# A range check on the row sums of a fused attention and FFN kernel, with a second path behind a branch

## The chip, the cores and the metric

The kernel runs on one core of one Trainium2 chip. The metric is device time in microseconds (us), the median of several runs. Beside it stands one execution taken by the hardware profiler; its span goes from the first to the last instruction of the program.

## What is computed

Eight sequences of 576 tokens with 8 heads of 64 are cut into chunks of 64 tokens. Each chunk attends to itself alone; the result goes through a multiplicative feed-forward network. Cut to what matters:

```python
scores = scale * np.matmul(q_c, k_c.transpose(0, 1, 2, 4, 3))
scores = scores - np.max(scores, axis=-1, keepdims=True)
attn = np.exp(scores)
attn = attn / (np.sum(attn, axis=-1, keepdims=True) + 1e-09)
out = np.matmul(attn, v_c)
# x: out as [4608 tokens, 512]; w1, w2: [512, 1024]; w3: [1024, 1024]; w_out: [1024, 512]
h = (x @ w1) * (x @ w2) @ w3
return h @ w_out
```

The inputs q, k and v are normal numbers times 0.1.

## The kernel before, in words

The 4608 tokens are worked in 18 parts p of 256 tokens (two units u of 128), and, from the products with w1 and w2 on, in 9 groups g = p // 2 of 512 tokens. The order of the work is written out by hand: the string ORDER names steps, each a letter with numbers, and the last lines of the kernel run them one after the other. Every instruction of a step is pinned in program order on its engine, so ORDER sets the queue of each engine. The steps that matter here:

- `q`, `k`, `v`, `i`, `o`, `h` load inputs and weights, issued by GpSimd (line 95). `T` (L197) transposes q and k on VectorE. `G` and `H` move tiles between partitions with DMAs that SP issues (line 189, `move`).
- `S`: scores on TensorE (all matmuls are recorded on line 92). `E` (L230): exp on ScalarE, straight from PSUM and without a maximum subtracted. `P`: products with v; a column of ones in v gives each row's sum beside them. `N` (L257, L260): VectorE takes the reciprocal of the sums (`rc`, 128x8) and multiplies. `X` (L272, L280): transposes for the network.
- `A`, `B`: products with w1 and w2 for eight slices j of the 1024 columns, `C` (L326): ScalarE copies the first out of PSUM into `a_sb`, `M` (L341): VectorE multiplies it with the second into `ab`. I write (12,5) for slice 5 of the group whose first part is 12.
- `V`, `W`, `Z` fold w3 and w_out into one matrix w3o, once. `O`: product of `ab` with it. `Y` (L371): ScalarE copies the result into `o_sb`; `Q`: SP stores it. The last part, O17, goes in three pieces (L364): two copies on ScalarE, and the last quarter on VectorE.

The sums, the scores, the pairs of products and the outputs share four PSUM tiles (`ps`, bufs=4) that rotate; `a_sb` has three buffers, `rc` two. The end of the kernel, in the order of ORDER, is the network of groups 12, 14 and 16 with the outputs between them: all attention is done before A12.1. After ORDER each engine branches to a closing block: SP waits on all semaphores, the engines meet, GpSimd clears the semaphores, and they meet again (recorded on line 449).

## Time and profile before

| what | value |
|---|---|
| median of 3 runs | 244.39 us (244.31 to 244.80) |
| span of the profiled execution | 243.1 us |
| granted TensorE clock | 1.000 |
| TensorE matmul busy | 225.9 us |
| VectorE busy | 153.7 us |
| ScalarE busy | 85.1 us |
| last matmul ends | 239.9 us |
| last copy (VectorE, L364) | 239.97, takes 0.42 us |

The runs are of the whole program; the profiled execution's time is known as its span, and what lies around it shows as the difference to the runs, 1.2 us. Engines are named PE (TensorE matmul), PEld (its weight load), DVE (VectorE), ACT (ScalarE), POOL (GpSimd) and SP (SyncE); a q behind a name is that engine's sequencer. In a timeline a row is start, duration, engine, line, operation and, in brackets, the idle time before it and what ended it. In a window table each pair is the busy time of an engine with its count, then the granted clock, the DMA engines' share and GB/s. In the list of a line, three numbers with slashes are the shortest, median and longest duration in ns, followed by the first and last start.

### The profile page before, as it was taken

The page shows a single profiled execution, that of the slowest core. Times are in us where ns is not written, and L with a number is a line of the kernel's source. Part 1 is how long each engine was busy: PE and PEld are TensorE (multiplying, and loading weights), DVE is VectorE, ACT ScalarE, POOL GpSimd, SP SyncE. Part 2 cuts the span into 40 slices and gives each one's busy share as a digit, 9 for nine tenths or more (in the row PEclk, how much of TensorE's full clock was granted, in tenths as well). Part 3 has the DMA queues.
Part 4 walks back from the last instruction along what each step waited for, and adds up shares of the span by engine and source line. Part 5 has one row for each costly group of instructions (what it writes and reads, how often), then busy time and mean ns, then how long its engine had stood idle before and what let it go on. Part 6 is the DMA issues. An engine that isn't in the chain of part 4 may idle for free.

```text
span 243.1 us, 6347 instructions
## 1 busy us (share of the span) xinstructions
PE 225.9 (93%) x2731; PEld 120.3 (49%) x2753; DVE 153.7 (63%) x232; ACT 85.1 (35%) x116; POOL 83.3 (34%) x112
## 2 busy tenths in 40 slices
PE   1299989999999979999999999999999999999994
PEld 1247868864545444444444444444444444444443
DVE  1856799689899578999998899918440332143000
ACT  2412323423333343534326335162332332332322
POOL 8847974665986444773260240000000000000000
PEclk9999999999999999999999999999999999999999
DMA  7999999999999999999999893735502200400244
GB/s 179 179 185 180 186 168 199 196 193 170 154 172 218 226 228 252 173 219 192 209 237 213 251 137 83 173 89 203 145 0 89 86 0 0 175 0 1 86 173 173
DMA packets 93595, 37.63 MB, mean 155 GB/s; under 512 B 75008, under 2 KB 86528, under 8 KB 93568
## 3 DMA queue, kind: packets, MB, share of 16 engines
q0 software_dynamic: 82592, 18.88, 83.9%
q1 hardware_dynamic: 9936, 17.83, 24.8%
q10 hardware_dynamic: 1040, 0.52, 0.8%
q8 instruction: 21, 0.34, 0.6%
q14 instruction: 6, 0.05, 0.1%
HBM read 38.80 MB, written 9.44 MB: 198 GB/s over the span
## 4 chain that ended last, share of the span: by engine, by line
PE 70%; DMA 16%; DVE 5%; SPq 3%; issue 2%; POOL 2%; ACT 0%; DVEq 0%; POOLq 0%
PE ab_ps L92 38%; PE o_ps L92 23%; PE w_ps L92 6%; DMA w<-in_moe_w_dram 4%; DMA qkm<-qkT 3%; DMA xt<-xm 3%; DMA qk<-in_k_dram 3%; DMA qk<-in_q_dram 3%; SPq L189 3%; PE s_ps L92 2%; PE pv L92 2%; DVE qkT L197 2%; DVE xn L260 1%; DVE ab L341 1%; POOL vbuf L95 1%
## 5 line engine op out<-in xcount | busy, mean ns | idle before, releaser
L92 PE MATMUL ab_ps<-xt,w 128*128 128x512 bf16 (+1 forms) x681 | 126.8, 342 | 1.4 <-DVE xt L272 0.9
L92 PEld LDWEIGHTS <-w 128*128 128x128 bf16 x704 | 67.3, 98 | 55.4 <-DVE xt L272 1.4
L341 DVE TENSOR_TENSOR ab<-a_sb,ab_ps 128x512 bf16<-128x512 f32 x71 | 47.8, 674 | 43.5 <-ACT a_sb L326 43.3
L326 ACT COPY a_sb<-ab_ps 128x512 f32<-128x512 f32 x71 | 41.6, 586 | 81.3 <-PE ab_ps L92 81.1
L92 PE MATMUL o_ps<-w3o,ab 128*128 128x512 bf16 (+1 forms) x285 | 63.3, 373 | 0.6
L197 DVE STREAM_TRANSPOSE qkT<-qk 128x1024 bf16<-128x1024 bf16 x36 | 45.1, 1289 | 8.0 <-ACT qk L140 5.5
L92 PEld LDWEIGHTS <-ab 128*128 128x128 bf16 x296 | 28.5, 98 | 32.3
L95 POOL DMA_DIRECT2D vbuf<-in_v_dram x40 | 33.9, 855 | 17.9 <-DMA qk<-in_k_dram 4.8
L371 ACT COPY o_sb<-o_ps 128x1024 f32<-128x1024 f32 x17 | 17.2, 1012 | 45.2 <-PE o_ps L92 41.3
L260 DVE TENSOR_TENSOR xn<-pv,rc 128x512 bf16<-128x512 f32 x36 | 24.9, 692 | 1.4
L95 POOL DMA_DIRECT2D qk<-in_q_dram x23 | 18.1, 790 | 9.9 <-DMA qk<-in_k_dram 3.1
L95 POOL DMA_DIRECT2D qk<-in_k_dram x23 | 18.0, 785 | 8.8 <-DMA vbuf<-in_v_dram 5.1
L230 ACT ACTIVATE e<-s_ps 128x1024 bf16<-128x1024 f32 x16 | 15.9, 1028 | 2.5 <-PE s_ps L92 2.2
L92 PE MATMUL w_ps<-wo,w3T 128*128 128x512 bf16 x62 | 13.9, 379 | 0.1
L280 DVE STREAM_TRANSPOSE xm<-xn 128x512 bf16<-128x512 bf16 x20 | 13.6, 697 | 0.2
L257 DVE RECIPROCAL rc<-pv 128x8 f32<-128x8 f32 x36 | 6.9, 192 | 9.9 <-PE pv L92 9.9
L95 POOL DMA_DIRECT2D w<-in_moe_w_dram x16 | 11.1, 697 | 5.8 <-DMA vbuf<-in_v_dram 2.3
L92 PEld LDWEIGHTS <-e 64*32 64x32 bf16 (+1 forms) x832 | 7.8, 97 | 8.5 <-issue 7.1
L272 DVE STREAM_TRANSPOSE xt<-xn 128x512 bf16<-128x512 bf16 x16 | 11.4, 711 | 0.5
L92 PE MATMUL pv<-vbuf,e 64*32 64x65 bf16 (+1 forms) x832 | 10.2, 198 | 1.5 <-ACT e L230 1.1
L92 PEld LDWEIGHTS <-qkT 32*64 32x64 bf16 x512 | 5.5, 117 | 11.0 <-DVE qkT L197 7.9
L364 DVE COPY o_sb<-o_ps 128x256 f32<-128x256 f32 x1 | 0.4, 425 | 16.0 <-PE o_ps L92 16.0
(24 smaller groups left out, 52.9 us busy)
## 6 DMA issues: line engine op xcount, KB each, us to landing
out_dram<-o_sb SPq DMA_DIRECT2D x17, 512.0 KB, 3.2
qkm<-qkT SPq DMA_DIRECT2D x40, 128.0 KB, 4.6
vbuf<-in_v_dram POOLq DMA_DIRECT2D x32, 128.0 KB, 8.6
w<-in_moe_w_dram POOLq DMA_DIRECT2D x16, 256.0 KB, 9.6
qk<-in_q_dram POOLq DMA_DIRECT2D x11, 256.0 KB, 6.9
qk<-in_k_dram POOLq DMA_DIRECT2D x11, 256.0 KB, 7.5
xt<-xm SPq DMA_DIRECT2D x40, 64.0 KB, 3.2
wo<-in_moe_w_out_dram POOLq DMA_DIRECT2D x4, 256.0 KB, 8.4
```

Of the source, the lines that this page charges most:

```text
L92: return inorder(nc.tensor.matmul(*a, **kw))
L95: return inorder(nc.gpsimd.dma_start(dst, src))
L189: inorder(nc.sync.dma_start(dst, src))
L197: inorder(nc.vector.transpose(qkT_t[g][:, :, p % 2, s, heads(h)].rearrange("p e h (y t) -> p h t e y", t=2), qk_t[p][:, s, heads(h)].rearr ...
L230: inorder(nc.scalar.activation(e_t[p][:, :, heads(hh)], s_t[p][:].rearrange("p u (h q) -> p u h q", q=CH)[:, :, heads(hh)], Exp, scale=sca ...
L257: inorder(nc.vector.reciprocal(rc[:], pv[:, :, :, D:W]))
L260: inorder(nc.vector.tensor_mul(xn_t[p][:, u], pv[:, :, :, 0:D], rc.to_broadcast([P, 2, 4, D])))
L272: inorder(nc.vector.transpose(new_xt(g)[:].rearrange("p (o t) -> p o t", o=KO)[:, :, t0:t0 + UT] .rearrange("p o (m y) -> p m o y", y=BL), ...
L280: inorder(nc.vector.transpose(xm_t[g][:, u, :, m].rearrange("p o (c y) -> p c o y", y=BL), xn_t[p][:].rearrange("p u r m d -> p (u r) m d" ...
L326: inorder(nc.scalar.copy(a_t[p, j][:], ps_t[p, j][:, 0, :]))
L341: inorder(nc.vector.tensor_mul(o, view(a_t.pop((p, j))[:]), view(ps_t.pop((p, j))[:, 1, :])))
L371: inorder(nc.scalar.copy(o_sb[:], ps_t.pop(p)[:]))
```

## The change

The reciprocals are kept in one constant tile `rcs` (128 x 288 f32) instead of two rotating ones. A step F, put between C12.5 and A12.6, tests all of them for lying between 2^-40 and 2^40: two comparisons, a product and a minimum on VectorE give one number for each partition, a DMA on SP moves the 128 numbers into one row, and VectorE sums the row and turns the sum into an integer, `flag`. A step L, put ahead of O16, loads the flag into a register of each of the five engines, with a check on SP that it lies from 0 to 128. After ORDER comes a branch on every engine: when the flag is below 128, a second path works all tokens again, with each row's maximum subtracted, and stores all outputs again. It is unrolled.

On VectorE step F's instructions stand between the product M of (12,4) and that of (12,5). The flag's load stands on SP right behind the move, on TensorE between the first weight load and the first matmul of O16, on ScalarE ahead of Y15's copy, on VectorE ahead of the very last copy, on GpSimd behind its last load. In the program the blocks lie in this order: the kernel; a short block for the path not taken, in which each engine waits for its own semaphore's last value and raises it to what the second path would have left (SP does it for the eight store queues), and then jumps to the closing block; the second path; the closing block. In it SP has twelve semaphore rows where it had nine, since the five sequencers' loads are waited for too.

```diff
-A12.5 M12.4 B12.5 C12.5 A12.6 M12.5 B12.6 C12.6 A12.7 M12.6 B12.7 C12.7 O9 M12.7 O10 Y9 Q9 A14.0 Y10
+A12.5 M12.4 B12.5 C12.5 F A12.6 M12.5 B12.6 C12.6 A12.7 M12.6 B12.7 C12.7 O9 M12.7 O10 Y9 Q9 A14.0 Y10
...
-C16.7 O13 M16.7 O14 Y13 Q13 O15 Y14 Q14 O16 Y15 Q15 Y16 Q16 O17
+C16.7 O13 M16.7 O14 Y13 Q13 O15 Y14 Q14 L O16 Y15 Q15 Y16 Q16 O17
...
+    rcs = consts.tile([P, 2 * NP, 2, 4, 1], f32, name="rcs")
+    flag = consts.tile([1, 1], mybir.dt.int32, name="flag")
...
+    def early(p):
+        return bool(rescue) or p < 8
...
-        rc = asb.tile([P, 2, 4, 1], f32, tag="rc", name="rc")
-        inorder(nc.vector.reciprocal(rc[:], pv[:, :, :, D:W]))
+        rc = rcs[:, 2 * p + u]
+        inorder(nc.vector.reciprocal(rc, pv[:, :, :, D:W]))
...
+    def do_F():
+        ge = consts.tile([P, NP * 16], f32, name="ge")
+        ok = consts.tile([P, NP * 16], f32, name="ok")
+        low = consts.tile([P, 1], f32, name="low")
+        row = consts.tile([1, P], f32, name="row")
+        n = consts.tile([1, 1], f32, name="n")
+        flat = rcs[:].rearrange("p u r m o -> p (u r m o)")
+        A = mybir.AluOpType
+        inorder(nc.vector.tensor_scalar(out=ge[:], in0=flat, scalar1=2.0 ** -40, scalar2=None, op0=A.is_ge))
+        inorder(nc.vector.tensor_scalar(out=ok[:], in0=flat, scalar1=2.0 ** 40, scalar2=None, op0=A.is_le))
+        inorder(nc.vector.tensor_mul(ok[:], ok[:], ge[:]))
+        inorder(nc.vector.tensor_reduce(out=low[:], in_=ok[:], op=A.min, axis=mybir.AxisListType.X))
+        move(row[:], low[:])
+        inorder(nc.vector.tensor_reduce(out=n[:], in_=row[:], op=A.add, axis=mybir.AxisListType.X))
+        inorder(nc.vector.tensor_copy(flag[:], n[:]))
+
+    def do_L():
+        whole.append(nc.values_load(flag[:], min_val=0, max_val=P))
+
+    def do_rescue():
+        rescue.append(True)
...
+        for g in range((NP + 1) // 2):
+            for p in (2 * g, 2 * g + 1):
+                load_qk(p, (0, 1))
+                load_v(p)
+                do_T(p, 0)
+                do_T(p, 1)
...
+                inorder(nc.vector.tensor_reduce(out=top[:], in_=s_v, op=mybir.AluOpType.max,
+                                                axis=mybir.AxisListType.X))
+                d = asb.tile([P, 2, H, CH], f32, tag="below", bufs=1, name="below")
+                inorder(nc.vector.tensor_sub(d[:], s_v, top[:].to_broadcast([P, 2, H, CH])))
...
+                do_P(p)
+                for u in range(2):
+                    do_N(p, u)
+                    do_X(p, u)
+            for j in range(FO):
+                do_A(2 * g, j)
...
+            for p in (2 * g, 2 * g + 1):
+                do_O(p)
+                do_Y(p)
+                do_Q(p)
...
     for step in ORDER.split():
         do[step[0]](*(int(n) for n in step[1:].split(".") if n))
+    with tc.If(whole[0] < P, preferred_fallthrough_block=False):
+        do_rescue()
```

More of the change, by code (lines that the diff above doesn't have):

```diff
@@ L7 @@
 from concourse._compat import with_exitstack
+from concourse.masks import make_identity
 ORDER = """
@@ L179, in load_wo, with paired @@
                  moe_w_out[i * DF // NB:(i + 1) * DF // NB].rearrange("(k x) n -> x k n", x=BL))
+    rescue = []
+    def early(p):
+        return bool(rescue) or p < 8
+    def paired(p):
+        return not rescue and p < 4
     half = [slice(0, CH), slice(CH, P)]
@@ L214, in do_S @@
         for h in range(H)[heads(hh)]:
-            if p < 8:
+            if early(p):
                 for e in range(2):
@@ L242, in do_P @@
             for m in range(4):
-                if p < 8:
+                if early(p):
                     for g in range(NB) if hh is None else (2 * hh, 2 * hh + 1):
@@ L269, in do_X @@
         g, m = divmod(p, 2)
-        if p < 8:
+        if early(p):
             t0 = m * PT + u * UT
@@ L301, in do_AB @@
     def do_AB(p, j, f, which):
-        if p >= 8:
+        if not early(p):
             rhs = new_xt(p // 2)[:].rearrange("p (s o t) -> p o s t", s=2, o=KO)
@@ L306, in do_AB @@
             rhs = new_xt(p // 2)[:].rearrange("p (o t) -> p o t", o=KO)
-            if p < 4:
+            if paired(p):
                 rhs = rhs[:, :, p % 2 * PT:(p % 2 + 1) * PT]
-        fs = (f,) if p >= 4 else (2 * j, 2 * j + 1)
+        fs = (2 * j, 2 * j + 1) if paired(p) else (f,)
         n = GT // len(fs)
@@ L331, in do_M @@
             ab_t[g] = msb.tile([P, FO, GT], bf, tag="ab", bufs=3, name="ab")
-        if p < 4:
+        if paired(p):
             o = ab_t[g][:, 2 * j:2 * j + 2, p % 2 * PT:(p % 2 + 1) * PT]
             view = lambda t: t.rearrange("p (j t) -> p j t", j=2)
-        elif p < 8:
+        elif early(p):
             o = ab_t[g][:, j]
@@ new lines @@
+    whole = []
+    def do_L():
+        whole.append(nc.values_load(flag[:], min_val=0, max_val=P))
+    def do_rescue():
+        rescue.append(True)
+        for t in (qkT_t, s_t, e_t, pv_t, xn_t, xt_t, qk_t, ab_t, ps_t, a_t, o_t):
+            t.clear()
+        ident = consts.tile([P, P], bf, name="ident")
+        make_identity(nc, ident[:])
+        for g in range((NP + 1) // 2):
[4 more added lines that the diff above has]
+                do_T(p, 1)
+                s_ps = psum("s_ps")
+                for h in range(H):
+                    for e in range(2):
+                        for i in range(NB):
+                            mm(s_ps[half[i % 2], i // 2, h * CH:(h + 1) * CH],
+                               lhsT=qkT_t[g][blk[i], e, p % 2, 0, h, :], rhs=qkT_t[g][blk[i], e, p % 2, 1, h, :],
+                               start=(e == 0), stop=(e == 1))
+                s_v = s_ps[:].rearrange("p u (h k) -> p u h k", k=CH)
+                top = asb.tile([P, 2, H, 1], f32, tag="top", bufs=1, name="top")
+                inorder(nc.vector.tensor_reduce(out=top[:], in_=s_v, op=mybir.AluOpType.max,
+                                                axis=mybir.AxisListType.X))
+                d = asb.tile([P, 2, H, CH], f32, tag="below", bufs=1, name="below")
+                inorder(nc.vector.tensor_sub(d[:], s_v, top[:].to_broadcast([P, 2, H, CH])))
+                en = asb.tile([P, 2, H, CH], bf, tag="en", bufs=1, name="en")
+                inorder(nc.scalar.activation(en[:], d[:], Exp, scale=scale, bias=0.0))
+                t_ps = ps.tile([P, 2, H, CH], bf, tag="p", name="t_ps")
+                for u in range(2):
+                    for h in range(H):
+                        for r in range(2):
+                            inorder(nc.tensor.transpose(t_ps[half[r], u, h, :], en[half[r], u, h, :],
+                                                        ident[half[r], half[r]]))
+                e_t[p] = asb.tile([P, 2, H, CH], bf, tag="e", bufs=2, name="e")
+                inorder(nc.scalar.copy(e_t[p][:], t_ps[:]))
+                do_P(p)
+                for u in range(2):
+                    do_N(p, u)
+                    do_X(p, u)
+            for j in range(FO):
+                do_A(2 * g, j)
+                do_B(2 * g, j)
+                do_C(2 * g, j)
+                do_M(2 * g, j)
+            for p in (2 * g, 2 * g + 1):
+                do_O(p)
+                do_Y(p)
+                do_Q(p)
@@ L420 @@
           "P": do_P, "N": do_N, "X": do_X, "A": do_A, "B": do_B, "C": do_C, "M": do_M, "D": do_D, "V": do_V,
-          "W": do_W, "Z": do_Z, "O": do_O, "Y": do_Y, "Q": do_Q}
+          "W": do_W, "Z": do_Z, "O": do_O, "Y": do_Y, "Q": do_Q, "F": do_F, "L": do_L}
     for step in ORDER.split():
         do[step[0]](*(int(n) for n in step[1:].split(".") if n))
+    with tc.If(whole[0] < P, preferred_fallthrough_block=False):
+        do_rescue()
 _INS = ['q', 'k', 'v', 'moe_w1', 'moe_w2', 'moe_w3', 'moe_w_out']
```

## The prediction

> **What bounds the kernel now.** I read the page first: TensorE is busy for 93% of the span at the full granted clock, and its slices are 9 from the second on but for one. Then the DMA queues, for the two rows of kind "instruction".

> ```profile
> PE 225.9 (93%) x2731; PEld 120.3 (49%) x2753; DVE 153.7 (63%) x232; ACT 85.1 (35%) x116; POOL 83.3 (34%) x112
> ...
> PE   1299989999999979999999999999999999999994
> ...
> DVE  1856799689899578999998899918440332143000
> ...
> q8 instruction: 21, 0.34, 0.6%
> ...
> q14 instruction: 6, 0.05, 0.1%
> ```

> From 167 us TensorE never waits; VectorE is nearly idle in the last slices. The instruction rows are code loads: 0.34 MB in 21 packets is 16 KB each, and 0.05 MB in 6 is 8 KB each. Next the chain that ended last, for the end:

> ```profile
> 222.86 10.74 PE o_ps L92 x49
> 233.60 0.05 issue
> 233.65 6.24 PE o_ps L92 x36
> 239.89 0.03 DVEq L364
> 239.93 0.04 issue
> 239.97 0.42 DVE o_sb L364
> ```

> TensorE ends at 239.89, VectorE copies the last quarter row (until 240.40), SP issues its store at 240.42, and 2.7 us of tail follow. Those are the rows of the closing line, L449:

> ```profile
> L449 SPq EVENT_SEMAPHORE  x11: 17/28/28, 240.8 to 243.1; - x11
> ...
> L449 SPq DRAIN  x3: 7/7/7, 242.3 to 242.6; - x3
> L449 PEldq DRAIN  x2: 13/1190/2368, 237.6 to 242.7; - x2
> ...
> L449 DVEq DRAIN  x2: 19/229/439, 240.0 to 242.7; - x2
> ```

> SP passes nine semaphore rows and two drains, then all engines meet. In the trace's records SP's row for the last store passes at 242.13 (the landing), the next two at 242.19 and 242.25, its drains at 242.32 and 242.38; the meeting is at 242.41 and the span ends at 243.15. So a satisfied row costs SP 0.063 us although it is busy for 0.028, and whatever comes after the landing, or arrives at the meeting after 242.4, is on the path.

> **Own time.** The span is 243.15; the three runs are 244.31 to 244.80, median 244.39. I work on the span and carry the 1.24 us around it over.

> **The change, part by part.** Nothing large is removed. The order of instructions ahead of step F is the same on every engine; the reciprocals go to a tile of their own with the same form (128x8, 192 ns) and the same waits: 0.

> *Step F* stands on VectorE between the product of (12,4) and that of (12,5). The views are VectorE's timeline and the window table around it:

> ```profile
> 176.63 0.69 DVE L341 TENSOR_TENSOR ab<-a_sb,ab_ps 128x512 bf16<-128x512 f32 x1 [1.04 <-ACT a_sb L326]
> 178.35 0.69 DVE L341 TENSOR_TENSOR ab<-a_sb,ab_ps 128x512 bf16<-128x512 f32 x1 [1.04 <-ACT a_sb L326]
> 180.08 0.69 DVE L341 TENSOR_TENSOR ab<-a_sb,ab_ps 128x512 bf16<-128x512 f32 x1 [1.04 <-ACT a_sb L326]
> 181.81 0.69 DVE L341 TENSOR_TENSOR ab<-a_sb,ab_ps 128x512 bf16<-128x512 f32 x1 [1.04 <-ACT a_sb L326]
> ```

> ```profile
> 176.00:178.00 2.00, 2.00 (x11) 0.91 (x10) 0.69 (x1) 0.85 (x2) 0.00 (x0) 1.00 0.00 0
> 178.00:180.00 2.00, 2.00 (x11) 0.94 (x10) 0.69 (x1) 0.86 (x2) 0.00 (x0) 1.00 0.00 0
> ```

> Four instructions over 288 f32 values start at 177.3. The nearest row below is the 128x256 memset (272 ns, so 0.31 at 288), above the 128x512 product (0.69): 1.2 to 2.8 us; I take 1.3, since 288 is near 256. Then SP's 512-byte move: the shortest landing of a move inside the chip is 1.9 us, the median 3.2, the longest 8.0; the DMA share here is 0.00 (last column but one), so 1.9. Two tiny ones, at most a reciprocal's 0.19 each: 0.4. VectorE waits for the move, and the product of (12,5) is queued behind: it starts at 177.3 + 1.3 + 1.9 + 0.4 = 180.9 instead of 178.35, ends at 181.6, and the next two, back to back, at 182.3 and 183.0. Who waits for them: TensorE has four PSUM tiles. (12,5), (12,6), (12,7) and O9 take all four; O9 (181.0 to 184.45) has the tile of (12,4), freed before F. O10 needs that of (12,5) at 184.45: slack 2.8 us. ScalarE's next a_sb need is at 189.8; ab of group 6 is read from 202 on. On SP the move and the flag's load stand ahead of O9's store, issued at 185.68. So F costs 0, between 0 and, with 2.8 and 8.0, 184.45 against 189.2: 4.8.

> *Step L* loads the flag into a register on five sequencers. No row shows such a load: from a TensorE semaphore row (0.05) to the shortest DMA round trip (1.7). On TensorE it stands before O16's first matmul, which started at 232.8. TensorE's sequencer runs ahead: its semaphore rows for A14 stand at 184.03 to 184.35, the matmul they guard runs at 187.9, so 3.5 us or more is queued and covers either price; 0 taken. Were that cover gone (the load waiting until the queue is empty), it would cost up to 1.7 plus a refill of some 0.2. ScalarE has 2.4 us idle between the output copies there, VectorE 16.0, GpSimd everything, SP 3 us before a store: 0.
> [...]

> *SP's end.* The path that is not taken still passes a block that raises each semaphore to what the second path would have left. On SP: eight semaphore rows for the store queues, a branch, then twelve rows (nine before, plus the five sequencers' own and others) and two drains. The rows up to the last store's are passed while it flies. After the landing stood two rows; now stand one, the branch, and twelve. That is 11 rows more at 0.063 = 0.69, and a branch at 0.05 to 0.3 (rows at the start bound it: between SP's start semaphore at 0.66 and its first DMA issue at 0.74 a branch already stands). I take 0.1. **+0.8**, and SP's part of the meeting is at 242.4 + 0.8 = 243.2.

> *The jump.* Unrolled, the second path is about 7,520 instructions on TensorE, 280 on VectorE, 190 on ScalarE, 150 on GpSimd, 40 on SP, and it lies between that block and the closing one. [...] They jump when their last work is done: TensorE at 240.0, ScalarE 239.5, VectorE 240.5. Price of a cold load: in the records VectorE's and ScalarE's 8 KB loads take 0.31 to 0.49 us, TensorE's 0.89 to 1.42. The last 8 KB one starts at 220.20, and ScalarE's sequencer, whose spacing fits it, last moved at 219.18 and before that at 217.46; so trigger to packet is 1.0 to 2.7. A load is 1.3 to 3.3 us on VectorE (2.7 + 0.49, rounded up). A jump can't be served sooner than a load that is ordered ahead, so I go near the upper end, 3.0: VectorE is at the meeting at 240.5 + 3.0 + 0.05 = 243.55, TensorE, 0.5 earlier and up to 0.9 longer to load, about the same. SP would be there at 243.2; **+0.4** more, between 0 and +0.7, and up to +4 if the closing block lies across a block's edge and a second load follows in series.
> [...]

> **Sum.** 0 + 0 + 0.8 + 0.4 = 1.2 us: span 244.35, time 245.6.

> **Rivals.**
> *Tail hidden: not slower.* Place: SP's rows after the last landing. If a satisfied row costs SP its busy time, 0.028, and not the 0.063 of its spacing, 11 are 0.3, the branch 0.1 and the load under 2.7: +0.4, 244.8, within 0.2%. It decides below 0.035 a row. Against it: nine rows in a row keep 0.06 to 0.07. 10%, and 2% for a time that is lower through chance of placement (new tiles move the others in SBUF); no row speaks for a gain.
> *A long load:* two in series, or one that takes 4 us or more, sets the end: +2 to +4.5, 246.4 to 249. [...] Against: DMA is quiet then. 13%.
> *TensorE stalls:* the flag's load holds the queue until it is empty (+1.9 with the rest: 247.5), or F's move takes over 4.7 us and holds O10 (to +4.8). Against: the lead of 3.5 us and the DMA share of 0.00. 5%.
> *Not what it says:* the second path runs. Sums of 64 exponentials of small numbers are near 64, the reciprocals near 2^-6, far inside 2^-40 to 2^40. Then it would be hundreds of us; under 1%.

> **Numbers.** The forecast has 70%: +0.5 to +2.0, 244.9 to 246.4. The range of 8 in 10 takes in half of the long loads and of the stalls: 244.9 to 247.4. A measurement here can tell 0.2%, 0.49 us: under 243.9 is faster (0.02), up to 244.88 the same (0.10), above that slower (0.88).

> **What would show it.** Right: TensorE's stages until 240 unchanged, its end at 239.9; the product of (12,5) late by about 2.5 us and nobody waiting; after the last store's landing 13 rows on SP; code packets of queues 8 and 14 after 240. Wrong: a gap in TensorE before O10 or O16 (F or L); VectorE's or TensorE's closing drain before SP's (the load is hidden and the sum is 245.2) or over 1 us after it (a long load); a last row before 242.6.

## The result and the profile after

The changed kernel takes 247.52 us (median of 4 runs, 247.20 to 248.27) against 244.59 us (244.31 to 245.36) for the kernel before in the same series: ratio 1.0120, 95% interval 1.0097 to 1.0143. The forecast was 245.6 in a range of 244.9 to 247.4: the sign is right, the size is less than half of what came. The profiled execution took 247.63 us with a span of 246.1.

First the page of the changed kernel: the engines' busy times, TensorE's slices, and the two rows of code loads.

```profile
PE 225.8 (92%) x2731; PEld 120.3 (49%) x2753; DVE 155.3 (63%) x238; ACT 85.2 (35%) x116; POOL 83.2 (34%) x112
...
PE   1289989999999999999999999999999999999990
...
q8 instruction: 23, 0.38, 0.6%
q14 instruction: 10, 0.08, 0.1%
```

TensorE's work is the same and its gap is only at the end: all the time that was added lies behind the last matmul, which ends at 239.84 (before: 239.88). There are two more 16 KB code packets and four more of 8 KB than before (23 and 10 against 21 and 6). Five of the six come after 240 us; the sixth, of 8 KB at 184.04, follows GpSimd's own jump at 182.70, long before the end. The chain of waits is of no help here: it holds VectorE's last copy alone and isn't followed back, so I read the rows of the two lines that end the program. First the branch (L507, in it the not-taken block); three numbers are shortest, median and longest duration in ns, then first and last start.

```profile
L507 SPq EVENT_SEMAPHORE  x8: 17/17/17, 240.9 to 243.8; - x8
...
L507 PEldq COMPARE_BRANCH  x2: 91/2038/3985, 237.5 to 240.0; - x2
L507 ACTq COMPARE_BRANCH  x2: 38/42/45, 239.0 to 239.5; - x2
L507 DVEq COMPARE_BRANCH  x2: 51/53/55, 240.0 to 240.5; - x2
L507 SPq COMPARE_BRANCH  x2: 38/44/49, 240.8 to 243.9; - x2
```

Each engine shown has two: the compare, and the jump from the not-taken block to the closing one. TensorE's compare takes 91 ns and its jump 3,985. VectorE's jump is recorded with some 0.05 us, but its next row, the first drain of the closing line (an engine's first row there), comes 3.1 us later:

```profile
L534 SPq EVENT_SEMAPHORE  x14: 17/28/28, 244.1 to 245.6; - x14
...
L534 ACTq DRAIN  x2: 8/44/81, 239.9 to 245.1; - x2
L534 DVEq DRAIN  x2: 10/34/58, 243.6 to 245.2; - x2
L534 PEldq DRAIN  x2: 8/40/73, 244.1 to 245.2; - x2
...
L534 DVEq EVENT_SEMAPHORE  x2: 21/21/21, 245.1 to 246.0; - x2
L534 PEldq EVENT_SEMAPHORE  x2: 51/51/51, 245.1 to 245.7; - x2
```

The first drains show when each engine reaches the closing block: ScalarE at 239.9 (0.45 after its jump), VectorE at 243.6, TensorE at 244.1. SP gets there at 244.1 too, some 1.7 us later than its rows alone would take it. The view of waits by engine says why; its columns are the total, the number and the longest wait.

```profile
SPq L507 <- SPq L507: 2.6, 2, 2.2
SPq L534 <- PEq L534: 0.7, 2, 0.5
```

In the not-taken block SP waits 2.2 us for the last store's semaphore. In the records the store is issued at 240.38 (before: 240.42); 15 of its 16 parts have landed by 242.29, the sixteenth at 243.72. Before, all 16 landed from 241.96 to 242.11. The DMA view from 240 to 247 us, in 40 slices, shows the same. The kernel before, then the changed one:

```profile
GB/s 363 386 363 328 310 41 0 234 345 170 0 0 0 0 0 0 0 0 0 0 0 0 0 0 0 0 0 0 0 0 0 0 0 0 0 0 0 0 0 0
```

```profile
GB/s 374 398 316 316 258 152 23 257 310 141 18 0 0 0 6 6 12 18 6 0 0 0 0 0 47 0 94 0 0 0 0 0 0 0 0 0 0 0 94 0
```

From 242.5 to 243.3 some 6 to 18 GB/s trickle: the eight 1 KB packets of the sixteenth part, behind a code packet of 16 KB on queue 8 that began at 240.96 and took 1.62 us. The first of the eight starts at 242.55, as the code packet ends (242.58). The records name no DMA engine for a packet; that the two share one I infer from these times, and in the three other runs whose TensorE jumps at this place (below: the changed kernel again, VectorE's edge moved, only TensorE's code long) the held part also starts within 0.03 us of the code packet's end. The packets at 244 and later are code again.

Where the 2.93 us between the medians lie, by the two profiled executions, counted from the end of the last matmul:

| from the last matmul's end, us | before | after | more |
|---|---|---|---|
| SP's row for the last store | 2.25 | 3.90 | +1.65 |
| from there to the meeting (GpSimd's first closing row) | 0.28 | 1.18 | +0.90 |
| from the meeting to the end | 0.74 | 1.14 | +0.40 |
| end of the span | 3.27 | 6.22 | +2.95 |

The last +0.40 is VectorE's: its final row stands at 246.0 (246.03 in the records), those of the other engines at 245.65, behind a second code load (an 8 KB packet at 244.20).

### The profile page after: what moved, and what is told of

Same layout as the page of the kernel before. It is cut to its first block, busy times and chain, and to the rows that moved or that the text cites. A ratio compares the mean times of both kernels' runs of the same rounds, so it can differ in the third digit from the quotient of the medians.

```text
span 246.1 us, 6392 instructions
## 1 busy us (share of the span) xinstructions
PE 225.8 (92%) x2731; PEld 120.3 (49%) x2753; DVE 155.3 (63%) x238; ACT 85.2 (35%) x116; POOL 83.2 (34%) x112
## 5 line engine op out<-in xcount | busy, mean ns | idle before, releaser
L271 DVE TENSOR_TENSOR xn<-pv,rcs 128x512 bf16<-128x512 f32 x36 | 24.9, 691 | 1.4
L268 DVE RECIPROCAL rcs<-pv 128x8 f32<-128x8 f32 x36 | 6.9, 192 | 10.4 <-PE pv L93 10.4
```

What stands on the lines that cost most here:

```text
L268: inorder(nc.vector.reciprocal(rc, pv[:, :, :, D:W]))
L271: inorder(nc.vector.tensor_mul(xn_t[p][:, u], pv[:, :, :, 0:D], rc.to_broadcast([P, 2, 4, D])))
```

## The experiments

My theory after the result, read from the code packets behind the jumps (from 240.96 to 244.67, where the kernel before has none after 220.20): an engine that jumps over the second path waits for such a packet, and each of three late things comes from these loads: TensorE's 16 KB packet (240.96, 1.62 us long) delays one sixteenth of the last store; the time from the jump to the next row (4.0 and 3.1 us); VectorE's last row, 0.38 us behind the others' (246.03 against 245.65), waits for a second 8 KB packet (244.20), as I took it because its closing instructions lie across the edge between two. The rival: raising the store queues' semaphores while the store flies, and the longer closing, cost the time, and the loads only happen beside them. All positions below are counted from the end of the last matmul, since the start of the span moves by up to 0.8 us between programs. A position is that of one profiled execution, a time the median of 4 to 12 runs, and the two agree only roughly: with only VectorE's code long the end is 1.16 us later than with only TensorE's, while the medians are 0.13 apart. Ratios are to the kernel before in the same series, with 95% intervals.

| kernel | ratio | last store's row on SP | meeting | end |
|---|---|---|---|---|
| before | 1 | 2.25 | 2.53 | 3.27 |
| no branch | 0.9988 (0.9973 to 1.0003) | 2.26 | 2.47 | 3.25 |
| small path | 1.0042 (1.0028 to 1.0056) | 2.26 | 3.44 | 4.22 |
| only TensorE's code long | 1.0107 (1.0088 to 1.0127) | 3.64 | 4.82 | 5.60 |
| only VectorE's code long | 1.0115 (1.0097 to 1.0132) | 2.26 | 4.23 | 6.76 |
| changed kernel | 1.0120 (1.0097 to 1.0143) | 3.90 | 5.08 | 6.22 |
| changed kernel, again | 1.0097 (1.0078 to 1.0116) | 3.72 | 4.90 | 6.20 |
| VectorE's edge moved | 1.0118 (1.0097 to 1.0138) | 3.91 | 5.09 | 5.89 |
| second path first | 1.0104 (1.0087 to 1.0122) | 3.43 | 4.39 | 5.78 |
| the same, edge moved | 1.0131 (1.0094 to 1.0168) | 3.58 | 4.54 | 5.34 |
| the same, with hints | 1.0106 (1.0088 to 1.0125) | 4.01 | 4.97 | 5.77 |
| hints, all jump late | 1.0099 (1.0063 to 1.0135) | 2.50 | 5.22 | 6.01 |
| hint, TensorE jumps late | 1.0056 (1.0034 to 1.0079) | 2.77 | 3.73 | 4.52 |

**No branch.** Steps F and L without the branch.

```diff
-    with tc.If(whole[0] < P, preferred_fallthrough_block=False):
-        do_rescue()
```

> Steps F and L stay, the branch and the second path are left out. Prediction's terms: F and L cost 0, and SP has three closing rows more than before at 0.063: end 3.4 after the last matmul against 3.24, time 0.2 above the kernel before (ratio 1.001). If F or L holds TensorE or the closing, the last matmul ends later than 239.9 or the time is 0.5 or more above.

The time can't be told from the kernel before (244.53 against 244.79 us), so F costs nothing. Of step L only SP's load is in this program; the other four engines have a semaphore row in its place. That TensorE's load costs nothing shows in the changed kernel, where no two matmuls after 170 us are more than 0.06 us apart. The three further closing rows, expected to cost 0.2, cost nothing either: SP passes them while the store flies, and the landing sits on the second to last row here.

**Small path.** The branch, the raised semaphores and the closing stay; the path behind the branch is a few instructions, and what it would compute is left out.

```diff
     def do_rescue():
         rescue.append(True)
...
+        z = psum("stub_ps")
+        mm(z[:, 0, 0:64], lhsT=zero[:, 0:P], rhs=zero[:, 0:64], start=True, stop=True)
+        for n in range(8):
+            load(vbuf[0][:, 0, :, 0:D], v[0, :, 0:2 * CH, :].rearrange("h p d -> p h d"))
+            move(out[NT - (n + 1) * P:NT - n * P, :], st[:])
```

> The branch, the raised semaphores, the flag's loads and the three further closing rows stay; the second path shrinks to 3 instructions on TensorE, 2 on VectorE and ScalarE, 17 on GpSimd and 13 on SP, so what it would compute is left out. Far jumps (code loaded after the jump is the cost): TensorE's and VectorE's jumps take under 0.3 us instead of 3.99 and 3.1, the last store lands at 242.15 as before instead of 243.7, SP is at the meeting 1.15 us later (243.3), and the span ends 0.74 after that, 244.05; time near 245.4. Rows and semaphores (the raising of the store queues' semaphores while the store flies is what delays its landing, the loads only happen beside it): landing stays at 243.7, the meeting at 244.9, time 247.1 to 247.5.

The rows of its branch line:

```profile
L469 SPq EVENT_SEMAPHORE  x8: 17/17/17, 240.3 to 241.6; - x8
...
L469 PEldq COMPARE_BRANCH  x2: 90/135/180, 236.9 to 239.5; - x2
```

and SP's wait in it:

```profile
SPq L469 <- SPq L469: 0.8, 1, 0.8
```

TensorE's jump is 180 ns instead of 3,985, VectorE's drain follows its jump by 0.2 us, no code packet comes after 220 us, and SP waits 0.8 us for the store instead of 2.2. The time is 1.0 us over the kernel before by the ratio (0.9 by the medians), and 0.9 of it are SP's rows between landing and meeting. So the rival falls: with the same rows and semaphores the store's row stands at 2.26, as in the kernel before (2.25), when the path behind the branch is short. The rest, 1.9 us, comes with the length of that path.

**Which engine's code.** The small path again, once with 3,750 repeated matmuls, once with 280 repeated memsets.

```diff
+        for _ in range(3750):
+            mm(z[:, 0, 0:64], lhsT=zero[:, 0:P], rhs=zero[:, 0:64], start=True, stop=True)
```

> The small second path (what it would compute is left out), but with 3,750 repeated matmuls in it, 7,503 instructions, so that TensorE's closing block alone is far away. Times from the last matmul's end, where the changed kernel stores land at 3.82, meet at 5.0 and end at 6.15, and the kernel before ends at 3.24 and the small path at 4.17. TensorE's load shares a DMA engine with the stores: its jump takes 4.0 us, the last store lands at about 3.8, SP's rows bring the meeting to 5.0 and the end to 5.75; time 1.6 us above the small path. If VectorE's packets delay the store, or the load does not touch it: landing 2.25, TensorE at the meeting at 4.2, end 4.9, 0.7 above the small path.

Its branch line and SP's wait in it:

```profile
L471 PEldq COMPARE_BRANCH  x2: 95/1906/3717, 237.7 to 240.2; - x2
```

```profile
SPq L471 <- SPq L471: 2.2, 1, 2.2
```

TensorE's load alone brings back the late landing: 3.64, with SP's wait of 2.2 us. No packet of queue 14 comes after 221 us in this run, so the packet of 16 KB (at 1.15, 1.45 us long) is what delays the store.

```diff
+        for _ in range(280):
+            inorder(nc.vector.memset(tick[:], 0.0))
```

> The small second path with 280 repeated memsets on VectorE (282 instructions, as many as the whole path had), so that VectorE's closing block alone is far away and lies across the same 8 KB edge as in the changed kernel. From the last matmul's end: the store lands at 2.25 as before, SP is ready at 3.4, VectorE's first load is over at 3.7, and its second one, 2.4 later, holds the end to 6.1: nearly as late as the changed kernel, with a different cause. If one load suffices: end 4.5. If VectorE's loads cost nothing: 4.17.

The closing line of this kernel, whose last matmul ends at 239.47:

```profile
L498 DVEq DRAIN  x2: 10/34/58, 243.6 to 243.9; - x2
...
L498 DVEq EVENT_SEMAPHORE  x2: 21/21/21, 243.8 to 246.2; - x2
L498 PEldq EVENT_SEMAPHORE  x2: 51/51/51, 243.8 to 244.4; - x2
```

The store lands on time, VectorE reaches the closing block 3.5 us after its jump, and its very last row comes 1.8 us after everyone else's, behind a second load. One of the two loads costs 0.8 at the meeting (4.23 against 3.44), the other 1.8 at the end. So the changed kernel holds two causes of which each alone makes about the whole loss, by the ratios: +2.6 with TensorE's code, +2.8 with VectorE's, +2.4 to +2.9 with both. They lie side by side, not one behind the other.

**VectorE's edge moved.** The changed kernel with 24 instructions more on VectorE in the path that doesn't run.

```diff
+        for _ in range(24):
+            inorder(nc.vector.memset(tick[:], 0.0))
```

> The changed kernel with 24 more VectorE instructions at the end of the second path, which is not run, so that VectorE's closing instructions do not lie across an 8 KB edge. If VectorE's last row (246.03, the other engines 245.65) is late by a second code load in series: one packet of queue 14 fewer after 240, VectorE's last row at 245.65, span 245.7, time 0.37 lower, near 247.15. If that row is late for another reason (the meeting's order): nothing changes, 247.5.

In the profile VectorE's last row is level with the others and the end is at 5.89 instead of 6.22, as expected. One packet of queue 14 is missing, but not the one at 244.20: that one comes here too, at 244.28, and the missing one is one of two at 246.7, after the last row. So a second 8 KB packet comes in both kernels, and VectorE's last row is behind the others' in one alone (by 0.38 us); that VectorE waits for the packet in the one kernel and not in the other is my reading. The medians (247.69 here, 247.52 for the changed kernel) don't show it: the runs spread by 1.2 us, and 0.33 can't be told.

**Second path first.** The far jump becomes the compare itself, which TensorE's sequencer reaches 2.3 us before the last matmul ends.

```diff
-    with tc.If(whole[0] < P, preferred_fallthrough_block=False):
+    with tc.If(whole[0] < P, preferred_fallthrough_block=True):
```

> The second path follows the compare directly and the not-taken block lies behind it, beside the closing block. The far jump is then the compare itself, which TensorE's sequencer reaches at 237.5, 2.5 us before its last matmul ends, and VectorE's at 240.0 instead of 240.5. Far jumps: TensorE's load (4.0) is over at 241.5, under its last matmuls, its packet is past before the last store is issued at 240.38, the store lands at 242.15, SP meets at 243.3; VectorE's first load is over at 243.1, and if its closing instructions still lie across an edge the second load (2.4 after the first) holds the end to 245.5: span 245.5, time 246.9; without that, 244.05 and 245.4. If a jump ahead of a busy engine is not served until the engine's queue is empty: TensorE again at 244, no gain, 247.5.

> As the kernel with the second path first, and 24 more VectorE instructions at the end of the path that is not run. Far jumps: both loads hidden or level with SP (VectorE 243.1, SP 243.3), one VectorE load only, span 244.05, time near 245.4, and so 2 us under the changed kernel; the 0.9 of SP's rows stays. If the loads are not the cause: 247 or more.

The rows of the branch line of the first of the two:

```profile
L507 SPq EVENT_SEMAPHORE  x8: 17/17/17, 241.1 to 243.5; - x8
...
L507 PEldq COMPARE_BRANCH  x1: 3955/3955/3955, 237.7 to 237.7; - x1
```

Both expectations missed (247.33 and 247.53 us). The load is indeed served while the matmuls run (compare at 237.7, next row at 241.7), but the store still lands late, at 3.43. I had looked at the last store alone. Its code packet came at 238.62, and then one part of sixteen lagged in all four last stores: their last completions came 1.8, 1.8, 1.4 and 1.2 us behind the median one. That this part shares its DMA engine with the code packet I infer from the times, as above. SP's issue of the third of them took 0.83 us instead of 0.34 as well, and that store's median part came at 1.70 instead of 1.38; why the issue took longer isn't shown. Why the part doesn't catch up I read from the window table of the kernel before (the last two columns are DMA share and GB/s):

```profile
238.00:240.00 2.00, 1.88 (x17) 1.44 (x15) 0.03 (x1) 0.96 (x2) 0.00 (x0) 1.00 0.81 302
240.00:241.00 1.00, 0.00 (x0) 0.00 (x0) 0.40 (x1) 0.00 (x0) 0.00 (x0) 1.00 0.90 313
241.00:242.00 1.00, 0.00 (x0) 0.00 (x0) 0.00 (x0) 0.00 (x0) 0.00 (x0) 1.00 0.39 131
```

The DMA engines are 81 to 90% busy from 238 to 241 us and 39% in the microsecond after it. In the run with the second path first, the delay taken on at 238.62 was still 1.2 us in the last store.

**A hint.** I put a prefetch hint for the branch (its rows, BRANCH_PREFETCH_HINT, stand below) behind the flag's load on TensorE and VectorE, with the register as its source, the second path first, the edge moved.

```diff
+        tc.mark_branch_hint_location('second', whole[0] < P, engines=[mybir.EngineType.PE, mybir.EngineType.DVE])
...
-    with tc.If(whole[0] < P, preferred_fallthrough_block=False):
+    with tc.If(whole[0] >= P, preferred_fallthrough_block=False, label="second") as good:
+        pass
+    with good.Else():
         do_rescue()
```

> The second path first in the program, 24 more VectorE instructions at its end, and a prefetch hint for the branch on TensorE and VectorE behind the load of the flag, with the register as its source, so some 8 us ahead of TensorE's compare. If the load after the jump is the cause and a hint moves it: code packets of queues 8 and 14 near 229 and 181 us, while the DMA share is 0.27 and 0.00; both jumps under 0.3 us; the last store lands 2.25 after the last matmul, SP's rows end at 3.4, the program at 4.2, as with the small path, although the second path is whole: ratio 1.004. If the hint does nothing: end 5.3 to 5.9, as with the second path first alone. If the hint's target is thrown out by the loads that follow in order: the same as if it did nothing, with packets twice.

Its branch line and the hints' rows in the closing line:

```profile
L512 SPq EVENT_SEMAPHORE  x8: 17/17/17, 241.3 to 243.6; - x8
...
L512 PEldq COMPARE_BRANCH  x1: 403/403/403, 237.2 to 237.2; - x1
```

```profile
L541 DVEq BRANCH_PREFETCH_HINT  x1: 60/60/60, 182.2 to 182.2; - x1
L541 PEldq BRANCH_PREFETCH_HINT  x1: 44/44/44, 229.3 to 229.3; - x1
```

On TensorE the hint works: a packet comes at 230.31, 1.0 us after the hint's row, and the jump takes 0.40 us where it took 4.10 without a hint (the second path first, the edge moved). Yet nothing is gained, since another packet comes 1.05 us after the jump: it takes 1.80 us, at 238.27, in the middle of the stores, and the last one lands at 4.01. SP's issue of the third store takes 1.35 us here, so the last one is also issued 0.46 us later than in the kernel before. On VectorE the hint does nothing: its jump is at 0.12, its next row at 3.23, 3.1 us later as in the changed kernel. The one packet of queue 14 near its hint, at 182.59, comes without a hint too (at 183.00 with the second path first), each time 1.1 us after GpSimd's jump.

**Jump late.** If what counts is when the packet comes, TensorE should jump when the stores' data has gone. First for all engines, by a flag that VectorE copies behind its last copy, with both hints from a first copy (their rows stand at 224.4). This kernel and the next have the second path first and the edge moved, like the hinted one.

```diff
+        inorder(nc.vector.tensor_copy(flag1[:], flag[:]))
+        early = nc.values_load(flag1[:], engines=engines)
+        tc.mark_branch_hint_location("second", early < P, engines=engines)
...
+        inorder(nc.vector.tensor_copy(flag2[:], flag[:]))
+        whole.append(nc.values_load(flag2[:], min_val=0, max_val=P))
```

> The whole second path, hinted on TensorE and VectorE as before, but the hint's flag is copied behind the last product (12,5)-like step of group 16, so both hints stand near 223 us, and the branch's flag is copied on VectorE behind its very last copy, so that no engine jumps before 0.7 us after the last matmul. Times from the last matmul's end. Theory (code packets in the stores' time are the cost): TensorE's compare at 1.35 takes 0.4 as with the hint before, the packet of the block that follows comes after 2.3, when the last store's data has gone; the store lands at 2.25; VectorE's hint, now close to its jump, saves its 3.1; SP's rows end at 3.4, the program at 4.2 to 4.3, time 245.5 to 245.9, ratio 1.004. If VectorE's hint does nothing again: VectorE at the meeting at 4.5, end 5.3, ratio 1.008. If the landing depends on the branch itself and not on when the packet comes: landing 3.6 to 4, end 5.7 to 6.

Its branch line:

```profile
L518 DVEq COMPARE_BRANCH  x1: 90/90/90, 240.6 to 240.6; - x1
L518 PEldq COMPARE_BRANCH  x1: 395/395/395, 240.6 to 240.6; - x1
...
L518 DVEq EVENT_SEMAPHORE  x1: 21/21/21, 244.5 to 244.5; - x1
```

The store lands at 2.23, as in the kernel before, with the packet behind TensorE's jump now at 2.09. That is the theory's main point. But VectorE's hint failed again (TensorE's brought a packet at 225.63, and no packet of queue 14 comes between the hint and 241.7), its load took 3.8 us from a later jump, and the end is set by it: half hit, half miss. So the last version leaves VectorE's jump where it was and holds TensorE alone, with the hint, behind three one-element copies on ScalarE.

```diff
+        tc.mark_branch_hint_location("second", whole[0] < P, engines=(mybir.EngineType.PE,))
...
+        for _ in range(3):
+            inorder(nc.scalar.copy(late[:], o_t[NP - 1][0:1, 1, DM - 1:DM]))
+        nc.values_load(late[:], engines=(mybir.EngineType.PE,))
```

> The whole second path, first in the program; VectorE jumps as soon as its last copy is handed over; TensorE has the hint at 229 us and waits, ahead of its compare, for three one-element copies on ScalarE behind VectorE's last copy, so it jumps 1.2 to 1.3 us after the last matmul. Theory: TensorE's compare takes 0.4, its follow-on packet comes after 2.2, the last store lands at 2.25 as in the kernel before, VectorE's load from its jump at 0.12 is over at 3.3, SP's rows at 3.4, the end is 4.2 after the last matmul (after the change 6.15): ratio 1.004, some 2 us under the changed kernel. If VectorE's load is slower for the packets beside it: up to 4 and an end of 4.9, ratio 1.007. If the theory is wrong and a far branch costs what it costs wherever its packets fall: 5.7 or more, ratio 1.010.

> The changed kernel once more, beside the last one, since its repeats spread by 1 us: 247.5, ratio 1.012; landing at 3.8 and end at 6.15 after the last matmul. A landing within 0.3 of the kernel before's would say that the shared DMA engine is a matter of chance.

Its branch line:

```profile
L517 SPq EVENT_SEMAPHORE  x8: 17/17/17, 241.0 to 242.8; - x8
...
L517 PEldq COMPARE_BRANCH  x1: 400/400/400, 241.3 to 241.3; - x1
...
L517 DVEq EVENT_SEMAPHORE  x1: 21/21/21, 243.1 to 243.1; - x1
```

246.29 us against 247.33 for the changed kernel in the same series: 1.0 us back with the whole second path in place, half of the 2 us that the theory gave; in the profiles the end moves by 1.7, from 6.20 to 4.52. The changed kernel itself came as it was expected again, with its store's row at 3.72. The packet behind TensorE's jump comes at 2.45, and VectorE is level with SP's rows. The store's row stands at 2.77 and not 2.25: one of its 16 parts is 0.5 us behind. An 8 KB packet lies at 241.11 beside it, 1.1 us after VectorE's jump. That it is the reason I infer and haven't tested; the record speaks for it, since in the changed kernel, where 8 KB packets begin at 1.20 and 1.91, two further parts of the store come late (2.42 and 2.45), and with only TensorE's code long, where there are none, no other part does (2.25 at most). No version with a far second path reaches the kernel before.

## Why the prediction was wrong

- **What bounds the kernel, and step F at 0:** right. The four instructions took 0.30, 0.30, 0.46 and 0.45 us (1.5 from start to end, where I took 1.3), the move 2.0 (1.9), the two small ones 0.4 (0.4). The waiting product started at 181.09 (180.9), and nobody waited for it:

```profile
177.19 0.30 DVE L417 TENSOR_SCALAR ge<-rcs 128x288 f32<-128x288 f32 x1
...
178.24 0.45 DVE L420 TENSOR_REDUCE low<-ok 128x1 f32<-128x288 f32 x1
180.71 0.27 DVE L422 TENSOR_REDUCE n<-row 1x1 f32<-1x128 f32 x1 [2.02 <-DMA row<-low]
181.02 0.14 DVE L423 CAST flag<-n 1x1 int32<-1x1 f32 x1
181.09 1.86 DVE L352 TENSOR_TENSOR ab<-a_sb,ab_ps 128x512 bf16<-128x512 f32 x3
```

- **Step L at 0:** right. The loads took 0.47 to 0.55 us; TensorE's stood at 228.9 and the matmuls went on without a gap.
- **SP's end, +0.8:** right in kind and size: 0.90, and 0.9 again with the small path. The branch took 0.19 of SP's time where I took 0.1.
- **The flight of the last store, put at nothing:** here the prediction failed. It counted the loads only as waits of the engines that jump. It has "The rows up to the last store's are passed while it flies" and takes that flight as it was before; the run shows that TensorE's packet makes the flight 1.65 us longer, and the landing carries all of SP's rows behind it. The sentence "DMA is quiet then", set against the rival of a long load, is what hid it: the window table above shows a share of 0.90 until 241 us and 0.39 in the microsecond after it. The packet began at 240.96, so it met the last store, and one part of sixteen is enough.
- **The jump, +0.4:** the sum was 0 + 0.8 + 0.4 for flight, SP's rows and loads; measured are 1.65 + 0.90 + 0.40. That the last terms agree is chance. The prediction's was a wait at the meeting for the first loads, but VectorE (3.77 after the last matmul) and TensorE (4.23) were there before SP (5.05), so it is 0; the measured one is VectorE's second load behind the meeting. The prediction had named this order of arrival as the sign of a hidden load and a sum of 245.2. The sign came and the time was 247.5, since SP was late itself. That the closing code comes by a load after the jump was an assumption of mine; the five code packets after 240 us show it, and in the small path, where none comes after 220 us, TensorE's jump takes 0.18. The load on VectorE was sized well (3.0 taken, 3.1 measured), but also by luck: it was made up of up to 2.7 before the packet and 0.49 for it, and the run has 1.2 before it, 0.39 for it, and 1.5 from its end to the next row, a part that the prediction didn't have. That a jump can't be served sooner than a load ordered ahead, by which I chose 3.0, was an assumption that no run shows: the 1.2 lies near the lower end of the 1.0 to 2.7 that I had estimated for a load ordered ahead.
- **TensorE's load "about the same" as VectorE's:** it reached the closing block at 244.07, not 243.55, since its load took 4.0 us. This was hidden behind SP, but would have been the bound without the late landing, by my estimate from the small path, where the meeting is at 3.44 against TensorE's 4.23 here.
- **"Up to +4 if the closing block lies across a block's edge":** no run shows where the code is divided; a second 8 KB packet (244.20) and VectorE's last row behind the others' did come. That cost 0.3 to 0.4 in the changed kernel, where, as I read it, the late landing covers most of it, and 1.8 where it stood alone (only VectorE's code long). I had given the long load 13% in all; the total, +2.9, is in the range stated for it, though more than half (1.65) came by another way.
- **The wait after a jump:** in the runs the jumps over the long path on TensorE and VectorE, without a hint that brought a packet, were 2.9 to 4.1 us ahead of the next row; ScalarE's in the changed kernel, over the 190 instructions that the prediction counts, 0.45. The larger part of the loss in the changed kernel (1.65 of 2.95) was not this wait of an engine that branches but the store that was held up.

## What to carry to other kernels

Here a jump over a long path had two prices: the engine's own wait (2.9 to 4.1 us), and a code packet, behind which one sixteenth of the stores under way was late (by 1.1 to 2.4 us against the median part, in the stores that 16 KB packets met). Before you call a load hidden, read the DMA share in the windows where it falls, and count what waits for all sixteen parts. When several late things lie side by side, removing one can show little in the time (here TensorE's code alone made +2.6 us, VectorE's alone +2.8, both +2.4 to +2.9): test each alone in a kernel that has none of the others.
